# Token blocks of 2, 2, 4, 4, 4 tiles in place of 2, 2, 3, 3, 3, 3, with four down accumulators and a ring of three PSUM banks

## The chip, the cores and the metric

The kernel runs on one core of a Trainium2 chip. The metric is the device time of one execution in microseconds. Before the change the runs took 521.86 us in the median of three (521.49 to 524.5). All compute engines of the core work side by side, each with its own in-order queue: TensorE (PE in the profile, with its weight loads as PEld), VectorE (DVE), ScalarE (ACT), GpSimd (POOL) and SyncE (SP), which issues the DMAs.

## What is computed

Two branches, each added to a residual stream x of 2048 tokens by 448 channels, with layer norms whose shift, scale and gate come from a condition c. The first branch is a long convolution of the tokens with a kernel K, the second a SwiGLU feed-forward network (FFN) of hidden width 1792:

```python
h = layernorm(x) * (1 + ca) + sa
x = x + ga * (conv(h, K) + h * Dskip)
h = layernorm(x) * (1 + cb) + sb
x = x + gb * ((silu(h @ w_gate) * (h @ w_up)) @ w_down)
```

For the inputs at hand the exponents in K are so small that K[l] = m0 + l m1, and the convolution becomes prefix sums over the tokens: a triangular matrix `tri` is multiplied with two products of h, and one row `run` carries what the earlier tokens leave to a tile.

## The kernel before

**Tiles and blocks.** The tokens lie in 16 tiles of 128 (on the partitions). The tiles are grouped in blocks (`BLOCKS`, line 23): 2, 2, 3, 3, 3 and 3 tiles. The FFN is worked block by block (`ffn`, from line 649, called at line 774). The hidden width is cut in 14 pieces f of 128. For each piece, `gate_up` (from line 664) multiplies the 448 channels of the block's tokens with the gate and up weights into two PSUM banks: 22 matmuls (line 678), each with as many columns as the block has tokens, 256 or 384. There are 22 because tokens and weights are kept as two float32r parts, `hhi`/`hlo` and the parts in `gu`. ACT then takes the silu of the gate bank (L684), DVE multiplies it with the up bank (L689, reads PSUM), ACT casts the product to `phi` (L692), and DVE keeps the rest in `plo` (L693). The down weights are split in `wdh` (ACT, L659) and `wdl` (POOL, L660) for each block and piece again. `down` (L704) multiplies them, 3 matmuls of 448 columns for each tile, into one accumulator bank for each tile: `dn0`, `dn1`, `dn2`.

**Order on PE.** PE runs gate_up(f), then down(f - 1), then gate_up(f + 1) and so on (loop at line 706). So the chain silu, product, cast, rest of piece f is meant to run beside PE's next work.

**The next block beside it.** While a block's FFN runs, the tiles of the next block are brought up to it. This work is in stages s0 to s5 for each tile (from line 780): s0 the first norm (DVE, L178 and L180); s1 the products v0 and v1 (POOL, L791 and L792); s2 adds the row `run` to both (DVE L797, POOL L798), casts `vh` (ACT, L801) and keeps the rest `vl` (DVE, L802); s3 the skip term (POOL, L807); s4 the three `tri` matmuls (PE, L813 to L815) into the bank `cv` and a bank `s` of the ring, and an addition (DVE, L816); s5 reads `o` and `s` (ACT L823, DVE L824, L826, L827) and passes `run` on through a small DMA (L825), which the next tile's s2 waits for. Then follow the second norm's statistics (L119, L120), its root for the block's tiles together (a guess on DVE, L125 to L128, Newton's steps on POOL, L134 to L137), the scaled tokens `xn` (DVE, L189), and, behind the last gate_up of the block, the transposes (PE, L196). These put each of the four channel groups k in a bank of the ring, from where ACT and DVE read `hhi` (L198), `fl` (L202 on DVE for k = 0 and 2, L200 on ACT for 1 and 3) and `hlo` (L203).

**What sets the order.** It is written by hand. `TIMES` (line 28) says in which half piece h each stage is emitted: h // 2 is the piece f; an even h stands between gate_up(f) and down(f - 1), an odd one behind down(f - 1). Its first row is for the work beside block 0, the second for that beside block 1, the third for all later blocks. In each row come the root of the first norm, then s0 to s5 for each tile, the root of the second norm, and `xn`. Every engine takes its instructions in this order.

**PSUM.** There are eight banks: four in a ring (`psg`, line 51, handed out in turn by `bank()`), three accumulators, and `cv`; `dn2` also serves the beginning.

**The beginning.** Until about 45 us the kernel's coefficients and the first two tiles are worked out. Block 0 runs while the FFN's weights come in and are split.

Of the kernel before, what the change touches and what calls it, by code (L numbers as in the profile page):

```python
# [17 lines left out]
NT = L // 128          # token tiles  # L18
P = 112                # partitions that the channels are spread over, four on each
NF = F // 128          # tiles of the hidden width  # L20
NP0 = 3                # pieces of the FFN's weights loaded before the branch
NS = 3                 # pieces on their way at a time
BLOCKS = [2, 2, 3, 3, 3, 3]
TILES = [list(range(sum(BLOCKS[:b]), sum(BLOCKS[:b + 1]))) for b in range(len(BLOCKS))]
MB = max(BLOCKS)
# when the root of the next block's first norm, the stages of its tiles, and the root and the shift
# of its second norm run, in half pieces of the hidden width: for the first block, the second, and those that follow
TIMES = (
# [3 lines left out]
)  # L32
EPS = 1e-5
# with exponents per step below this (here: the root of the sum of their squares), exp(l dt A) is
# 1 + l dt A to float32's accuracy for every l < L
# [8 lines left out]
def tile_kernel(ctx, tc, x, a_re, a_im, b_re, b_im, c_re, c_im, log_dt, dskip,  # L44
                wg, wu, wd, c, w_mod, dft, idft, out):
    nc = tc.nc
# [4 lines left out]
    psg = ctx.enter_context(tc.tile_pool(name="psg", bufs=4, space=PS))  # L51
# [16 lines left out]
    # ---- weights of the FFN, one tile of the hidden width at a time: gate and up are kept as  # L68
    # two float32r parts each (for the last 64 channels on top of each other), down whole ----
# [29 lines left out]
    tok = const.tile([128, 1], F32)     # a token's place in its tile  # L99
    run = const.tile([128, 2, D], F32)  # row 0: what the tokens so far leave to a tile, see s1  # L100
# [4 lines left out]
    gm1 = g0                        # the general path works the gates out again  # L105
# [16 lines left out]
    def guess(v, n, tag):  # L122
        """the beginning of 1 / sqrt(v + eps): a first guess from the bits, for Newton's steps"""
        a, w, y, t = (small.tile([128, n], F32, name=q + tag) for q in "awyt")
        ve.tensor_scalar(a, v, EPS, None, op0=OP.add)  # L125
        ve.tensor_scalar(w, v, EPS, -0.5, op0=OP.add, op1=OP.mult)
        ve.tensor_scalar(y.bitcast(I32), a.bitcast(I32), 1, None, op0=OP.logical_shift_right)
        ve.tensor_scalar(y.bitcast(I32), y.bitcast(I32), -1, 0x5F3759DF, op0=OP.mult, op1=OP.add)  # L128
        return w, y, t
# [15 lines left out]
    class Norm:  # L145
        """mean and 1 / deviation of the tokens of a block's tiles"""
# [69 lines left out]
    # the sum over the four channels of a partition  # L216
# [11 lines left out]
    def end_gate():  # L228
        """the sum over the partitions, on every partition"""
        ps = psd.tile([128, 512], F32, name="dn2")[:, 0:D]  # L230
        pe.matmul(ps, ones[0:P, :].to_broadcast([P, 128]), gb[0:P], start=True, stop=True)
        sc.copy(gb, ps)

    def mod_col(col, row, bias):
        """sums over a row's partitions as columns, the last 64 channels twice"""
        pc = bank()
        for q, o in ((0, 0), (1, 0), (2, 0), (3, 0), (3, 64)):
            n = 128 if q < 3 else 64
            pe.matmul(pc[o:o + n, q:q + 1], row[:, q * 128:q * 128 + n], ones[0:row.shape[0], :], start=True, stop=True)
        sc.activation(col, pc[:, 0:4], AF.Identity, bias=bias)  # L240

    def row_of(m):
        """a row of the kernel on every partition"""
        ps = bank()
        for k in range(4):
            pe.matmul(ps[:, k * P:(k + 1) * P], m[:, k:k + 1].to_broadcast([P, 128]), ident[0:P, 0:P],
                      start=True, stop=True)
        return ps[:, 0:D].rearrange("q (k p) -> q p k", k=4)
# [5 lines left out]
    def warm(n):  # L254
        """keeps the tensor engine's clock up while it waits"""
        ps = bank()
        for _ in range(n):
            pe.matmul(ps.rearrange("p (a b) -> p a b", a=4), tri, tri[:, None, :].to_broadcast([128, 4, 128]),
                      start=True, stop=True)
# [4 lines left out]
    with tc.tile_pool(name="pre", bufs=1) as pre, tc.tile_pool(name="wm", bufs=6) as wm:  # L264
# [52 lines left out]
        # all ones, and the steps from a token of the first tile to one of the second  # L317
# [4 lines left out]
        # what the parts of both tiles leave to the third: column 0 at its first token, column 32 for  # L322
        # each step
# [24 lines left out]
        # K[d, l] for small exponents: m0 + l m1, with m0 = sum C dt B and m1 = sum C dt B dt A  # L348
# [37 lines left out]
        # the exponents of one step  # L386
# [10 lines left out]
        # the branch of the first tiles  # L397
# [52 lines left out]
        # v0 of the tiles to come has their own places taken off  # L450
# [6 lines left out]
    def general_conv():  # L457
        hd = dram.tile([L, D], F32, name="hd")
        kd = dram.tile([L, D], F32, name="kd")          # columns in the order (k p)
# [19 lines left out]
        with tc.tile_pool(name="kg", bufs=1) as kg:  # L479
            tr = {n: kg.tile([128, 2, D], F32, name="tr" + n) for n in ("rho", "th", "tc", "wr", "wi", "wn")}  # L480
            with tc.tile_pool(name="ka", bufs=1) as ka:
# [25 lines left out]
                # angles in turns; whole turns of a step (and of LF steps) drop out exactly  # L507
# [12 lines left out]
            with tc.tile_pool(name="ke", bufs=2) as ke, tc.tile_pool(name="kt", bufs=2) as kt:  # L520
# [9 lines left out]
                def powers(n, cnt, hf, d0, re, im):  # L530
                    """exp(l dt A) for the steps l of iot[n]: re and im are [128, DC, cnt]"""
                    sh = [128, DC, cnt]
                    io = iot[n][:, None, :].to_broadcast(sh)
                    th = tr["th" if n == "f" else "tc"][:, hf, d0:d0 + DC][:, :, None].to_broadcast(sh)
                    rh = tr["rho"][:, hf, d0:d0 + DC][:, :, None].to_broadcast(sh)
                    a = kt.tile(sh, F32, name="a" + n)
                    m = kt.tile(sh, F32, name="m" + n)
                    po.tensor_tensor(m, rh, io, op=OP.mult)
                    if n == "c":
                        sc.activation(m, m, AF.Exp, scale=float(LF))  # L540
                    else:
                        sc.activation(m, m, AF.Exp)
                    ve.tensor_tensor(a, th, io, op=OP.mult)
                    frac(a, re)
                    sc.activation(im, a, AF.Sin, scale=TURN)
                    ve.scalar_tensor_tensor(a, a, -1.0, a, op0=OP.mult, op1=OP.max)
                    sc.activation(re, a, AF.Sin, scale=-TURN, bias=half_pi)
                    po.tensor_tensor(im, im, m, op=OP.mult)
                    ve.tensor_tensor(re, re, m, op=OP.mult)

                for d0 in range(0, D, DC):
                    e2 = ke.tile([128, 2, 2, DC, LF], F32, name="e2")
                    e1 = ke.tile([128, 2, 2, DC, LC], F32, name="e1")
                    for hf in range(2):
# [7 lines left out]
                        # re(W e1) and -im(W e1)  # L562
# [15 lines left out]
        # blocks of 512 steps, transformed at the roots of z^512 = i: the real part of a  # L578
        # product's inverse is its low half, the imaginary part its high half
# [64 lines left out]
    def run_blocks(pools, st, first=None):  # L644
# [3 lines left out]
        def ffn(ts, fresh, last, todo):  # L648
# [5 lines left out]
            def split_d(j):  # L654
                if last:            # the gates of the end go into the weights
                    po.tensor_tensor(wdn[j], wdn[j], gb, op=OP.mult)
                hi = hid.tile([128, D], F32R, name="wdh")
                lo = hid.tile([128, D], F32R, name="wdl")
                sc.copy(hi, wdn[j])  # L659
                po.tensor_tensor(lo, wdn[j], f32(hi), op=OP.subtract)  # L660
                wp[j] = hi, lo

            def gate_up(f, nw):
                head = fresh and f == 0     # the tokens come in while it runs
# [8 lines left out]
                def mm(s, lo):  # L673
                    # the parts of the weights that meet each part of the tokens
# [42 lines left out]
            if last:                # one tile after the other  # L717
# [26 lines left out]
        for b, ts in enumerate(TILES):  # L744
            todo = {}
            if b + 1 < len(TILES):
# [18 lines left out]
                for n, (h, *hs) in ((n1, root1), (n2, root2)):  # L765
                    go(h, n.guess, nx)
                    for h in hs:        # on Pool if a step at a time
                        go(h, n.newton, nx, len(hs) > 1, 3 // len(hs))
# [7 lines left out]
    def small_path(pools):  # L776
# [8 lines left out]
        # K * h up to a token at place t of a tile: v0 and v1 are the parts of h at t = 0 and for  # L785
        # each step, so it is sum v0 + t sum v1. Row 0 brings in the tokens before the tile.
# [125 lines left out]
```

## Time and profile before

| what | value |
|---|---|
| median of the runs | 521.86 us (521.49 to 524.5) |
| span of the profiled execution, first to last instruction | 522.0 us |
| mean granted TensorE clock | 0.980 |
| PE busy | 489.4 us (94%) |
| DVE / ACT / POOL busy | 315.5 / 189.0 / 242.4 us |
| block 0, from 45 us to the first gate matmul of block 1 | until 122.7 us |
| block 1 | 122.7 to 188.0 us |
| blocks 2, 3, 4, 5 | begin at 188.0, 271.0, 354.0 and 436.9 us |

A row of the timeline gives start in us, duration in us, engine, line of the kernel, operation, out<-in, shape and count, and in brackets how long the engine had been idle and what released it. A row of the chain of waits gives start, duration, and the engine and line that held the end up. A row of the windows gives, for each engine, the busy time in a stretch, then the granted clock of TensorE and the DMA share. Matmuls overlap one another, so their pace is read from their starts and not from their durations.

### The profile page before, as it was taken

Reading aid. Unit: us, or ns where it says so; the run is one execution under the profiler, and the core shown is the slowest. Engines: PE = TensorE matmul, PEld = TensorE weight load, DVE = VectorE, ACT = ScalarE, POOL = GpSimd, SP = SyncE. Lnnn points to the kernel's source line nnn. Section 1 sums busy time; section 2 is a strip of 40 time slices with the busy share of each in tenths; the row PEclk is TensorE's granted clock in tenths of the full one; section 3 lists DMA queues with packets and bytes.
Section 4 is the critical chain, followed back from the end, with each engine's and each line's share of the span. In section 5 each row is a group of like instructions: output and inputs, shape, how many; then the busy total and the mean of one; then the engine's idle time right before and its main releaser. Section 6 shows DMA issues by size and latency. Waiting matters only on the chain.

```text
span 522.0 us, 7464 instructions
## 1 busy us (share of the span) xinstructions
PE 489.4 (94%) x2747; PEld 454.8 (87%) x2747; DVE 315.5 (60%) x598; ACT 189.0 (36%) x388; POOL 242.4 (46%) x293
## 2 busy tenths in 40 slices
PE   7768988789989899999999999999999999999995
PEld 4345877679979899999999999999999999999995
DVE  3889889986877764577285466557367538221122
ACT  4346743534333342333243233333233324232221
POOL 1676494552566513565312566311548433434430
PEclk9879999998998989999999999999999999999999
DMA  7995554402000020000003000003000001000001
GB/s 209 277 217 158 157 168 140 122 22 89 0 2 1 2 89 0 1 1 3 1 5 101 0 2 0 2 0 107 1 0 2 0 1 54 1 1 0 2 0 60
DMA packets 25862, 26.08 MB, mean 50 GB/s; under 512 B 2232, under 2 KB 25144, under 8 KB 25816
## 3 DMA queue, kind: packets, MB, share of 16 engines
q1 hardware_dynamic: 25816, 25.52, 17.2%
q8 instruction: 23, 0.38, 0.3%
q14 instruction: 23, 0.19, 0.1%
HBM read 21.80 MB, written 3.67 MB: 49 GB/s over the span
## 4 chain that ended last, share of the span: by engine, by line
PE 73%; DVE 15%; issue 4%; ACT 2%; POOL 2%; DMA 2%; SPq 1%; DVEq 0%; ACTq 0%; POOLq 0%
PE bank L678 46%; PE dn L704 23%; DMA bi<-in_A_B_im_dram 2%; DVE plo L693 2%; DVE gu L95 1%; PE bank L196 1%; DVE xn L189 1%; DVE scr L359 1%; PE dn L415 1%; DVE stb L119 1%; DVE v L797 1%; DVE gu L93 1%; DVE x L816 1%; DVE x L827 1%; DVE wr L368 1%
## 5 line engine op out<-in xcount | busy, mean ns | idle before, releaser
L678 PE MATMUL bank<-hhi,gu 128*128 128x384 f32 (+1 forms) x1169 | 212.6, 321 | 0.5 <-DVE gu L95 0.4
L678 PEld LDWEIGHTS bank<-hhi,gu 128*128 128x128 f32 x1169 | 191.9, 189 | 4.4 <-DVE gu L95 0.6
L660 POOL TENSOR_TENSOR wdl<-wd,wdh 128x448 fp32r<-128x448 f32 x84 | 104.0, 1241 | 191.8 <-ACT wdh L659 183.2
L678 PE MATMUL bank<-hlo,gu 128*128 128x384 f32 (+1 forms) x668 | 131.9, 319 | 0.0
L689 DVE TENSOR_TENSOR p<-p,bank 128x384 f32<-128x384 f32 (+1 forms) x84 | 42.6, 507 | 126.9 <-PE bank L678 122.5
L678 PEld LDWEIGHTS bank<-hlo,gu 128*128 128x128 f32 x668 | 110.1, 189 | 0.0
L692 ACT CAST phi<-p 128x384 fp32r<-128x384 f32 (+1 forms) x84 | 40.1, 477 | 160.2 <-DVE p L689 160.1
L693 DVE TENSOR_TENSOR plo<-p,phi 128x384 fp32r<-128x384 f32 (+1 forms) x84 | 54.5, 649 | 40.5 <-ACT phi L692 40.5
L704 PE MATMUL dn<-wdh,phi 128*128 128x448 f32 x224 | 61.8, 376 | 3.5 <-ACT phi L692 3.4
L684 ACT ACTIVATE p<-bank 128x384 f32<-128x384 f32 (+1 forms) x83 | 37.8, 455 | 71.3 <-PE bank L678 71.2
L704 PE MATMUL dn<-wdh,plo 128*128 128x448 f32 x224 | 60.9, 372 | 2.7 <-DVE plo L693 2.7
L704 PE MATMUL dn<-wdl,phi 128*128 128x448 f32 x224 | 61.0, 373 | 1.5 <-POOL wdl L660 1.5
L659 ACT CAST wdh<-wd 128x448 fp32r<-128x448 f32 x84 | 47.6, 566 | 31.3 <-PE dn L704 28.3
L704 PEld LDWEIGHTS dn<-wdh,plo 128*128 128x128 f32 x224 | 42.5, 191 | 7.8 <-DVE plo L693 4.2
L704 PEld LDWEIGHTS dn<-wdl,phi 128*128 128x128 f32 x224 | 42.9, 192 | 6.1 <-POOL wdl L660 2.3
L704 PEld LDWEIGHTS dn<-wdh,phi 128*128 128x128 f32 x224 | 40.4, 192 | 5.9 <-ACT phi L692 4.5
L791 POOL TENSOR_TENSOR v<-h,gm 128x448 f32<-128x448 f32 x14 | 16.4, 1169 | 12.7 <-DVE h L180 12.7
L801 ACT CAST vh<-v 128x448 fp32r<-128x448 f32 x14 | 7.9, 567 | 33.3 <-DVE v L797 33.3
L798 POOL TENSOR_TENSOR v<-v,run 1x448 fp32r<-1x448 f32 x14 | 17.4, 1240 | 2.3 <-DMA run<-run 1.3
L792 POOL TENSOR_TENSOR v<-h,g 128x448 fp32r<-128x448 f32 x14 | 18.2, 1297 | 0.0
L807 POOL TENSOR_TENSOR h<-h,gd 128x448 f32<-128x448 f32 x14 | 17.6, 1260 | 0.0
L189 DVE TENSOR_SCALAR xn<-x,mvb,yb 128x448 f32<-128x448 f32 (+1 forms) x28 | 16.1, 643 | 2.2 <-POOL yb L137 2.2
(182 smaller groups left out, 462.3 us busy)
## 6 DMA issues: line engine op xcount, KB each, us to landing
wmt<-in_w_mod_dram SPq DMA_DIRECT2D x6, 784.0 KB
x<-in_A_u_dram SPq DMA_DIRECT2D x16, 224.0 KB
out_dram<-x SPq DMA_DIRECT2D x16, 224.0 KB
wd<-in_B_w_down_dram SPq DMA_DIRECT2D x14, 224.0 KB
raw<-in_B_w_gate_dram SPq DMA_DIRECT2D x14, 192.0 KB
raw<-in_B_w_up_dram SPq DMA_DIRECT2D x14, 192.0 KB
raw<-in_B_w_gate_dram SPq DMA_DIRECT2D x14, 64.0 KB
raw<-in_B_w_up_dram SPq DMA_DIRECT2D x14, 64.0 KB
```

Of the source, the lines that this page charges most:

```text
L189: ve.tensor_scalar(xn[i][:, o:o + n], src[:, a:a + n], *n2.of[i], op0=OP.subtract, op1=OP.mult)
L659: sc.copy(hi, wdn[j])
L660: po.tensor_tensor(lo, wdn[j], f32(hi), op=OP.subtract)
L678: pe.matmul(ps[s][:, 0:n], w[:, s, a], (hlo if lo else hhi)[:, k, 0:n], start=not lo and a == 0, stop=lo and k == 3)
L684: sc.activation(p[:, 0:n], ps[0][:, 0:n], AF.Silu)
L689: ve.tensor_tensor(p[:, 0:n], p[:, 0:n], ps[1][:, 0:n], op=OP.mult)
L692: sc.copy(hi[:, 0:n], p[:, 0:n])
L693: ve.tensor_tensor(lo[:, 0:n], p[:, 0:n], f32(hi[:, 0:n]), op=OP.subtract)
L704: pe.matmul(dn[q][:, 0:D], u[:, cs], v, start=f == 0 and z == 0, stop=f == NF - 1 and z == 2)
L792: po.tensor_tensor(v1, h, gm1, op=OP.mult)
L798: po.tensor_tensor(v1[0:1], f32(v1[0:1]), run[0:1, 1, :], op=OP.add)
L807: po.tensor_tensor(h, h, gd, op=OP.mult)
```

## The change

The last twelve tiles are grouped by four, in three blocks in place of four. `MB` becomes 4, so that the tiles `hhi`, `hlo`, `p`, `phi`, `plo` grow from 384 to 512 columns, there are 8 buffers for x in place of 6 and 4 for `xn` in place of 3. A fourth accumulator `dn3` needs a bank, and the ring is cut to three. `TIMES` has four tiles in its second and third row, at a regular distance of four half pieces. A last line makes room on chip by a smaller scratch for DMAs that GpSimd would issue; the kernel has none. Comments are left out of the new file, which shifts its line numbers by two.

```diff
-BLOCKS = [2, 2, 3, 3, 3, 3]
+BLOCKS = [2, 2, 4, 4, 4]
...
 TIMES = (
     ((3, 3, 4, 4), (6, 8, 8, 9, 11, 11), (12, 14, 15, 17, 20, 20), (21, 22, 23, 23), (24, 25)),
-    ((3, 4), (6, 8, 9, 10, 10, 11), (10, 10, 13, 13, 15, 16), (15, 16, 18, 18, 21, 21), (21, 22, 22, 23), (24, 24, 24)),
-    ((3, 3, 3, 3), (7, 8, 8, 10, 10, 10), (10, 13, 13, 14, 14, 15), (14, 17, 17, 18, 18, 19), (19, 20, 21, 22), (24, 24, 24)),
+    ((3, 4), (5, 6, 6, 7, 8, 8), (8, 9, 10, 11, 12, 12), (12, 13, 14, 15, 16, 16), (16, 17, 18, 19, 20, 20),
+     (21, 22, 22, 23), (24, 24, 24, 24)),
+    ((3, 3, 3, 3), (5, 6, 6, 7, 8, 8), (8, 9, 10, 11, 12, 12), (12, 13, 14, 15, 16, 16), (16, 17, 18, 19, 20, 20),
+     (20, 21, 22, 23), (24, 24, 24, 24)),
 )
...
-    psg = ctx.enter_context(tc.tile_pool(name="psg", bufs=4, space=PS))
+    psg = ctx.enter_context(tc.tile_pool(name="psg", bufs=3, space=PS))
...
-    nc = bacc.Bacc("TRN2", target_bir_lowering=False, num_devices=1)
+    nc = bacc.Bacc("TRN2", target_bir_lowering=False, num_devices=1, dynamic_dma_scratch_size=1024)
```

## The prediction

> **What bounds the kernel now.** I read the page first, then the windows cut at the first gate matmul of each block, then the chain of waits, and at last the timeline of the places where the chain leaves PE.
>
> ```profile
> span 522.0 us, 7464 instructions
> PE 489.4 (94%) x2747; PEld 454.8 (87%) x2747; DVE 315.5 (60%) x598; ACT 189.0 (36%) x388; POOL 242.4 (46%) x293
> ```
>
> ```profile
> 122.70:188.00 65.30, 61.93 (x415) 57.54 (x414) 50.45 (x107) 24.31 (x54) 33.98 (x39) 0.95 0.06 19
> 188.00:271.00 83.00, 83.00 (x457) 80.97 (x456) 46.05 (x88) 27.64 (x54) 36.71 (x50) 1.00 0.05 15
> ...
> 354.00:436.90 82.90, 82.90 (x457) 80.74 (x456) 48.15 (x90) 27.37 (x54) 37.69 (x51) 1.00 0.05 18
> 436.90:522.00 85.10, 79.70 (x435) 77.27 (x433) 21.76 (x38) 21.35 (x42) 31.08 (x27) 1.00 0.05 18
> ```
>
> Blocks 2 to 4 have PE busy without a gap at clock 1.00, DVE a little over half of the time. There PE's pace is the time. Block 1 is different: 65.30 us, PE not always busy, clock 0.95, DVE 50.45 of 65.30. The profiled span (522.0) and the median (521.86) agree, so I add to 522.0.
>
> PE's pace comes from the chain of waits (a piece with 256 tokens, one with 384):
>
> ```profile
> 129.24 2.57 PE bank L678 x22
> 131.81 1.23 PE dn L704 x6
> ...
> 201.64 1.82 PE dn L704 x9
> 203.46 3.89 PE bank L678 x22
> ...
> 209.17 3.89 PE bank L678 x22
> 266.20 1.31 PE bank L196 x12
> ```
>
> A 384-token piece takes 209.17 - 203.46 = 5.71 us: 22 gate/up matmuls in 3.89 (176.8 ns each) and 9 down matmuls in 1.82 (202 ns each). With 256 tokens it is 2.57 (116.8 ns each) and 1.23, so 3.80 a piece. Fourteen pieces of 5.71, nine `tri` matmuls of about 0.2 and 1.31 of transposes make 83.1, the window's 83.0: a block's edge costs nothing beside its work.
>
> **The change part by part.**
>
> *Wider gate and up matmuls.* Gate/up matmuls in the last twelve tiles go from 4 x 14 x 22 = 1232 of 384 columns to 3 x 14 x 22 = 924 of 512. The work of 448 columns (down, transposes, `tri`) is per tile and stays. The timeline shows one run of 512-column matmuls on the same type, the warming ones, at clock 1.00; each row begins with the start of another of them:
>
> ```profile
> 13.63 0.85 PE L258 MATMUL bank<-tri 128*128 128x512 f32 x3
> 13.86 0.85 PE L258 MATMUL bank<-tri 128*128 128x512 f32 x3
> 14.09 0.84 PE L258 MATMUL bank<-tri 128*128 128x512 f32 x3
> 14.32 1.07 PE L258 MATMUL bank<-tri 128*128 128x512 f32 x4
> ```
>
> ```profile
> 13.50:14.00 0.50, 0.50 (x4) 0.41 (x3) 0.50 (x2) 0.00 (x0) 0.00 (x0) 1.00 0.99 287
> ```
>
> (14.32 - 13.63) / 3 = 230 ns; I take 229, since 448 columns at 202 and the step from 384 to 448 (25 ns for 64) lead there too. A third more columns than 384 would be 236 at proportional pace. So 22 x 0.229 = 5.04 where pro rata it is 3.89 x 4/3 = 5.19: 0.148 a piece, times 42 pieces: **-6.2 us**. Ends: 0 (236 ns) and, from 512 columns at the slope 448 to 384 without any fixed part (about 0.4 ns a column, some 213 ns), -20.
>
> *One tile more is prepared in block 1.* Blocks 2 and 3 prepare 8 tiles where blocks 2 to 4 prepared 9; its 0.6 of `tri` and 0.44 of transposes leave them: **-1.0 us**.
>
> *Block 1 with four tiles.* This is the term that decides. Block 1 still has 256 tokens and 14 pieces of 3.80, but must bring up four tiles. The marks are the starts of the subtraction `vl`, once for each tile:
>
> ```profile
> 143.40 0.87 DVE L802 TENSOR_TENSOR vl<-v,vh 128x448 fp32r<-128x448 f32 x1 [0.63 <-ACT vh L801]
> 155.74 0.63 DVE L802 TENSOR_TENSOR vl<-v,vh 128x448 fp32r<-128x448 f32 x1 [0.69 <-ACT vh L801]
> 155.75 0.47 PE L813 MATMUL cv<-vh,tri 128*128 128x448 f32 x1 [1.44 <-ACT vh L801]
> 169.39 0.63 DVE L802 TENSOR_TENSOR vl<-v,vh 128x448 fp32r<-128x448 f32 x1 [0.63 <-ACT vh L801]
> ```
>
> 12.34 and 13.65 us lie between them, though by `TIMES` (half pieces 9, 13, 18) only 2 and 2.5 pieces do, 7.6 and 9.5 us of PE. PE waits for the stages (row at 155.75). What fills the distance is DVE's queue, one after the other: product, cast wait, rest of two pieces, L816, L824, L826, L827, statistics, next tile's L178 and L180, L797, wait for `vh`, `vl`. Beside POOL some of these are stretched:
>
> ```profile
> 146.61 0.63 DVE L816 TENSOR_TENSOR x<-h,x 128x448 f32<-128x448 f32 x1 [1.05 <-POOL h L807]
> 152.09 1.13 POOL L798 TENSOR_TENSOR v<-v,run 1x448 fp32r<-1x448 f32 x1
> 152.37 1.21 DVE L693 TENSOR_TENSOR plo<-p,phi 128x256 fp32r<-128x256 f32 x1 [0.47 <-ACT phi L692]
> 153.50 1.55 DVE L797 TENSOR_TENSOR v<-v,run 1x448 f32<-1x448 f32 x1
> 157.38 0.43 DVE L693 TENSOR_TENSOR plo<-p,phi 128x256 fp32r<-128x256 f32 x1 [0.47 <-ACT phi L692]
> 168.15 0.61 DVE L797 TENSOR_TENSOR v<-v,run 1x448 f32<-1x448 f32 x1
> ```
>
> The same L693 takes 0.43 alone and 1.21 while POOL's L798 runs, L797 0.61 and 1.55. In the new `TIMES` the marks stand at half pieces 6, 10, 14 and 18: three distances of exactly 2 pieces, with the same DVE work as in the 12.34. Bounds for one: 12.34 less 0.78, 0.94 and the 1.05 wait is 9.6; above 13.65. I take 12.0, near the first distance, which has the same content; a little is taken off because s3 now stands ahead of POOL's next L660. PE offers 2 x 3.80 + 0.6 = 8.2 for it, so DVE stays behind and PE waits in each.
>
> Before the first mark lies the same time as before (143.40 - 122.7 = 20.7): a fourth column in the first norm's statistics and root, but one piece less. The last mark has its old place (18), and behind it come the same four pieces: 188.0 - 169.39 = 18.6, plus the fourth tile's `xn`:
>
> ```profile
> 179.34 3.66 DVE L189 TENSOR_SCALAR xn<-x,mvb,yb 128x448 f32<-128x448 f32 x6 [0.95 <-POOL yb L137]
> ```
>
> (3.66 / 3 = 1.2), and 1.5 for the shorter ring (product, cast, rest and `fl` follow `xn`, and the last transposes wait for them, next part): 21.3. So block 1 is 20.7 + 3 x 12.0 + 21.3 = 78.0, against 65.3: **+12.7 us** (5.5 to 17.7 by the bounds). Queued behind DVE are L689 and L693 of each piece, and PE's next down and gate matmuls wait for those.
>
> *Three banks.* The order of the changed program shows the ring: gate, up, then the four transposes take banks 0, 1, 2, 0, 1, 2. The third group waits for L689 on the up bank, the fourth for L198 and L202 to empty the first group's bank. Before, it had a bank of its own.
>
> ```profile
> 266.04 1.47 PE L196 MATMUL bank<-ident,xn 128*128 128x128 f32 x12
> 266.30 0.55 DVE L689 TENSOR_TENSOR p<-p,bank 128x384 f32<-128x384 f32 x1 [1.23 <-PE bank L196]
> 266.89 0.51 ACT L692 CAST phi<-p 128x384 fp32r<-128x384 f32 x1 [2.05 <-DVE p L689]
> 267.44 0.56 DVE L693 TENSOR_TENSOR plo<-p,phi 128x384 fp32r<-128x384 f32 x1 [0.58 <-ACT phi L692]
> 268.01 0.68 DVE L202 TENSOR_SCALAR p<-bank,cb1c,sbc 128x384 f32<-128x384 f32 x1
> ```
>
> L202 ends 2.65 us after the transposes' start. For 512 columns the four steps grow by about 0.5 (their growth from 256 to 384 columns, 0.13, 0.10, 0.14, 0.14): 3.15. Twelve transposes take 1.31, so PE stands 1.8 at the edges 2 to 3 and 3 to 4, and behind the transposes in its queue the last two down groups and the next block's gate matmuls. A stall of this size can cost clock behind it:
>
> ```profile
> 180.00:184.00 4.00, 2.50 (x20) 1.95 (x18) 3.53 (x8) 0.64 (x2) 1.66 (x2) 0.98 0.00 0
> 184.00:188.00 4.00, 4.00 (x15) 3.59 (x13) 3.60 (x8) 3.61 (x7) 0.31 (x1) 0.59 0.00 0
> 184.31 3.85 PE dn L704 x12
> ```
>
> After 1.5 us of idleness the clock was 0.59 and twelve down matmuls took 3.85 instead of 12 x 0.202 = 2.43, 1.4 lost. I charge it at one of the two edges: 2 x 1.8 + 1.4 = **+5.0 us** (0 to 6.4). At the edge of block 0:
>
> ```profile
> 117.91 0.99 PE L196 MATMUL bank<-ident,xn 128*128 128x128 f32 x7 [1.07 <-DVE xn L189]
> 118.66 0.82 PE L704 MATMUL dn<-wdh,phi 128*128 128x448 f32 x2
> 119.35 0.54 DVE L202 TENSOR_SCALAR p<-bank,cb1c,sbc 128x256 f32<-128x256 f32 x1
> ```
>
> the fourth group waits until 119.89 and the down matmuls begin 0.2 later, at 120.1 in place of 118.66: **+1.4 us** (0 to 1.4). Inside the pieces the ring makes gate(f + 2) wait for L827 where an s4 stands in piece f: in blocks 0 and 1 that falls inside waits already charged, in the wide blocks L827 has two pieces (15 us) for it.
>
> *At nothing.* Splits of down weights fall from 84 to 70 on ACT and POOL, off the path. SP issues 4 loads of x at a time; for blocks 3 and 4 they queue behind the stores of the same buffers, and are needed one piece (7.5 us) later. If that cover went, DVE would stand in L119 and L689 behind it. In the beginning the fourth transposes wait too; the cover is DVE's splitting of weights, and without it some 0.4 us. The end has one tile more to add, each beside the next tile's down matmuls.
>
> **Sum.** 522.0 - 6.2 - 1.0 + 12.7 + 5.0 + 1.4 = **533.9 us**.
>
> **The rivals.**
>
> *Not slower: the fourth tile fits in block 1.* DVE is idle for 65.3 - 50.45 = 14.9 us there, more than the 12.0 charged for a whole tile. Then block 1 grows by PE's own 1.0 alone, and the sum is 522.0 - 7.2 + 1.0 + 6.4 = 522.2. Against it: idle time between dependent steps was there before too, and the distance was still 12.3. It decides at 9.8 us a tile: below it the total stays within 1%.
>
> *512 columns run without the fixed part.* If a gate/up matmul took 216 ns in place of 229, it would be 924 x 13 = 12 us less: 521.9. For it: the slope from 384 to 448 columns; against it: the four rows above. The Trainium skill, "TensorE: Matmul & The Clock Gate", section "Wait — 56ns, not 53.3ns?", gives 2.5 ns beside the columns at 2.4 GHz, 215.7 ns for 512 columns; its estimate for 384 is 162.5, where this trace has 176.8, so it does not hold here.
>
> *Wider is only proportional* (236 ns): the -6.2 is gone, 540.1.
>
> *DVE and the clock are worse:* three distances of 13.65 (+5.0) and the clock lost at both edges (+1.4): 540.3. The Trainium skill, same page, section "A second HAM failure mode: psum-queue depth-cycling", speaks for it: waits for PSUM banks can make the clock swing. Blocks 2 to 4 at 1.00 show no such swing with four banks.
>
> **How the numbers follow.** Forecast 0.52; only proportional 0.10; worse 0.13; fourth tile fits 0.11; no fixed part 0.06; both of these last (about 510) 0.08. One per cent (516.8 to 527.2) is about what a measurement tells from no change. Faster is the last case, 0.08; within it are the two single ones, 0.17; slower the rest, 0.75. The range 521 to 543 leaves out the case at 510 and the two bad cases together (546.5); the forecast's own range is 527 to 541.
>
> **What would show it.** Block 1's window near 78 us, with `vl` starts some 12 us apart and PE's L813 waiting for `vh` at each of four tiles. Gate/up pieces of 512 tokens near 5.04 us. At the edges of the wide blocks 12 transposes, a gap of about 1.8 us ended by DVE L202, then 4 more. It is wrong if block 1 stays below 72 us, or if the wide pieces take 4.75 or 5.19.

## The result, and the profile after

The changed kernel takes 543.36 us in the median of four runs (542.84 to 547.14), the kernel before, on the same chip, 522.93 (521.49 to 524.5). The ratio is 1.0396, with a 95% interval of 1.0354 to 1.0437: the change makes the kernel 4% slower. The forecast was 533.9, and its range ended at 543. Line numbers of the changed kernel are those of the kernel before plus two (L693 is now L695).

The head of the page of the changed kernel, and its windows, cut again at the first gate matmul of each block (duration, then busy time of PE, PEld, DVE, ACT and POOL, then TensorE's granted clock):

```profile
span 541.3 us, 6691 instructions
...
PE 494.4 (91%) x2439; PEld 415.2 (77%) x2439; DVE 318.7 (59%) x561; ACT 175.7 (32%) x340; POOL 222.2 (41%) x255
```

```profile
124.92:204.78 79.86, 65.07 (x422) 60.45 (x421) 60.59 (x126) 26.12 (x56) 40.38 (x43) 0.91 0.06 18
204.78:316.85 112.07, 110.55 (x505) 93.23 (x505) 64.39 (x104) 32.60 (x56) 44.22 (x55) 1.00 0.04 13
316.85:428.92 112.07, 110.55 (x506) 93.21 (x505) 65.99 (x106) 32.07 (x55) 44.65 (x56) 1.00 0.05 17
428.92:541.30 112.38, 105.94 (x477) 88.96 (x475) 26.25 (x40) 24.31 (x41) 28.96 (x26) 0.99 0.05 18
```

Set beside the windows of the kernel before, this gives the whole difference of the spans, 541.3 - 522.0 = 19.3:

| stretch | before | after | difference | forecast |
|---|---|---|---|---|
| start to block 1 | 122.7 | 124.9 | +2.2 | +1.4 |
| block 1 | 65.3 | 79.9 | +14.6 | +12.7 |
| the last twelve tiles | 334.0 | 336.5 | +2.5 | -2.2 |
| sum | 522.0 | 541.3 | +19.3 | +11.9 |

So the loss sits in block 1, as forecast, and the wide blocks, which were to give something back, give nothing. The time of this profiled execution is 543.13, which is 1.8 above its span; the forecast added to a span of 522.0 as if it were a time. Of the distance from 533.9 to 543.1, 7.4 us are terms of the sum and 1.8 this base.

**The wide blocks.** The chain of waits of the changed kernel shows their pieces, and the edge between blocks 2 and 3 (start, duration, what held the end up):

```profile
217.49 5.13 PE bank L680 x22
222.63 2.43 PE dn L706 x12
225.06 5.13 PE bank L680 x22
...
308.43 0.68 DVE p L691
309.13 0.63 ACT phi L694
309.79 0.69 DVE plo L695
310.48 0.81 DVE p L204
311.33 0.66 PE bank L198 x4
311.99 4.86 PE dn L706 x24
```

A 512-column matmul steps by 5.13 / 22 = 233.2 ns, not 229; four thirds of the old 176.8 would be 235.7. The gain is 924 x 2.5 ns = 2.3 us, not 6.2. At the edge PE leaves the chain for DVE and ACT, exactly in the order that the forecast gave: product, cast, rest, then `fl` (L204), and only then the last four transposes. The window of 112.07 less 14 pieces of 7.565, 12 `tri` matmuls (2.4) and 16 transposes (1.75) leaves 2.0 us of standstill at such an edge. The 24 down matmuls behind it run at 202.5 ns: no clock is lost.

**Block 1.** The marks `vl`, and the PE, POOL and DVE rows around the second of them, in the timeline of the changed kernel:

```profile
146.20 0.85 DVE L804 TENSOR_TENSOR vl<-v,vh 128x448 fp32r<-128x448 f32 x1 [0.63 <-ACT vh L803]
157.70 0.79 DVE L804 TENSOR_TENSOR vl<-v,vh 128x448 fp32r<-128x448 f32 x1 [0.69 <-ACT vh L803]
170.22 0.79 DVE L804 TENSOR_TENSOR vl<-v,vh 128x448 fp32r<-128x448 f32 x1 [0.69 <-ACT vh L803]
182.75 0.79 DVE L804 TENSOR_TENSOR vl<-v,vh 128x448 fp32r<-128x448 f32 x1 [0.69 <-ACT vh L803]
```

```profile
157.72 0.47 PE L815 MATMUL cv<-vh,tri 128*128 128x448 f32 x1 [0.80 <-ACT vh L803]
159.53 0.47 PE L816 MATMUL bank<-v,tri 128*128 128x448 f32 x1 [1.34 <-POOL v L800]
```

```profile
154.09 1.16 POOL L793 TENSOR_TENSOR v<-h,gm 128x448 f32<-128x448 f32 x1 [4.76 <-DVE h L182]
155.21 1.33 POOL L794 TENSOR_TENSOR v<-h,g 128x448 fp32r<-128x448 f32 x1
156.50 1.51 POOL L662 TENSOR_TENSOR wdl<-wd,wdh 128x448 fp32r<-128x448 f32 x1
157.97 1.50 POOL L800 TENSOR_TENSOR v<-v,run 1x448 fp32r<-1x448 f32 x1
159.44 1.32 POOL L809 TENSOR_TENSOR h<-h,gd 128x448 f32<-128x448 f32 x1
```

```profile
160.80 1.56 DVE L818 TENSOR_TENSOR x<-h,x 128x448 f32<-128x448 f32 x1 [1.04 <-POOL h L809]
```

The distances are 11.50, 12.52 and 12.53. In the last two, the split of a down weight (POOL, L662) stands in POOL's queue between v1 and its row (L800). So L800 ends 1.5 us later, PE waits 1.34 in L816 behind a wait for `vh`, and DVE waits 1.04 in L818 for the skip term. The forecast had POOL's next split behind s3, and did not count the one ahead of L800. It also put the whole distance down to DVE's queue. In these two distances the chain goes over to POOL and back: L793 starts when DVE's `h` is done (L182), POOL works v0, v1, the split, v1's row and the skip term one after the other (154.09 to 160.76), and DVE's L818 waits for the last of them. Before the first mark lie 21.3 us, between the marks 36.6, behind the last 22.0: 79.9. TensorE's granted clock is 0.91 over the block, where it was 0.95 before.

**The end.** Behind the end of PE's last matmul the changed kernel's span lasts 6.5 us more, that of the kernel before 5.4: +1.1. There is one store more in the last block (four in place of three), but the run *What the 512 columns read* below has four as well, and lasts 5.4 us there. So the number of stores is not shown to be the reason; over the profiles of the changed tiling this stretch varies from 5.4 to 6.5.

### The profile page after: what moved, and what is told of

It is laid out like the page before. It is cut to its first block, busy times and chain, and to the rows that moved or that the text cites. A ratio compares the mean times of both kernels' runs of the same rounds, so it can differ in the third digit from the quotient of the medians.

```text
span 541.3 us, 6691 instructions
## 1 busy us (share of the span) xinstructions
PE 494.4 (91%) x2439; PEld 415.2 (77%) x2439; DVE 318.7 (59%) x561; ACT 175.7 (32%) x340; POOL 222.2 (41%) x255
## 4 chain that ended last, share of the span: by engine, by line
PE 69%; DVE 12%; POOL 7%; issue 5%; DMA 3%; ACT 2%; SPq 1%; POOLq 0%; ACTq 0%; DVEq 0%
PE bank L680 43%; PE dn L706 21%; POOL wdl L662 2%; DVE plo L695 2%; DVE xn L191 1%; DVE scr L361 1%; POOL v L800 1%; DMA x<-in_A_u_dram 1%; DMA dsk<-in_A_Dskip_dram 1%; PE bank L215 1%; DMA wd<-in_B_w_down_dram 1%; POOL v L794 1%; POOL v L793 1%; PE dn L417 1%; DVE gu L97 1%
## 5 line engine op out<-in xcount | busy, mean ns | idle before, releaser
L680 PE MATMUL bank<-hhi,gu 128*128 128x512 f32 (+1 forms) x973 | 206.9, 352 | 2.3 <-DVE x L829 1.2
L680 PEld LDWEIGHTS bank<-hhi,gu 128*128 128x128 f32 x973 | 162.6, 190 | 28.9 <-DVE x L829 1.4
L662 POOL TENSOR_TENSOR wdl<-wd,wdh 128x448 fp32r<-128x448 f32 x70 | 87.2, 1249 | 164.6 <-ACT wdh L661 160.9
L680 PE MATMUL bank<-hlo,gu 128*128 128x512 f32 (+1 forms) x556 | 126.5, 349 | 0.0
L691 DVE TENSOR_TENSOR p<-p,bank 128x512 f32<-128x512 f32 (+1 forms) x70 | 40.5, 579 | 138.9 <-PE bank L680 134.3
L680 PEld LDWEIGHTS bank<-hlo,gu 128*128 128x128 f32 x556 | 92.6, 188 | 15.4
L694 ACT CAST phi<-p 128x512 fp32r<-128x512 f32 (+1 forms) x70 | 37.4, 535 | 160.5 <-DVE p L691 160.5
L695 DVE TENSOR_TENSOR plo<-p,phi 128x512 fp32r<-128x512 f32 (+1 forms) x70 | 52.3, 748 | 36.9 <-ACT phi L694 36.9
L686 ACT ACTIVATE p<-bank 128x512 f32<-128x512 f32 (+1 forms) x69 | 35.4, 512 | 80.4 <-PE bank L680 80.4
L793 POOL TENSOR_TENSOR v<-h,gm 128x448 f32<-128x448 f32 x14 | 16.3, 1166 | 69.7 <-DVE h L182 69.7
L800 POOL TENSOR_TENSOR v<-v,run 1x448 fp32r<-1x448 f32 x14 | 20.3, 1453 | 0.4
L809 POOL TENSOR_TENSOR h<-h,gd 128x448 f32<-128x448 f32 x14 | 20.3, 1453 | 0.0
L215 PE MATMUL bank<-wmt,cs 112*128 112x448 f32 (+1 forms) x32 | 16.8, 683 | 2.9 <-DMA wmt<-in_w_mod_dram 2.9
```

What stands on the lines that cost most here:

```text
L215: pe.matmul(ps[0:rows, 0:D], cs[:, k:k + 1].to_broadcast([P, rows]), w[k], start=k == 0, stop=k == 3)
L680: pe.matmul(ps[s][:, 0:n], w[:, s, a], (hlo if lo else hhi)[:, k, 0:n], start=not lo and a == 0, stop=lo and k == 3)
L686: sc.activation(p[:, 0:n], ps[0][:, 0:n], AF.Silu)
L691: ve.tensor_tensor(p[:, 0:n], p[:, 0:n], ps[1][:, 0:n], op=OP.mult)
L694: sc.copy(hi[:, 0:n], p[:, 0:n])
L695: ve.tensor_tensor(lo[:, 0:n], p[:, 0:n], f32(hi[:, 0:n]), op=OP.subtract)
```

## The experiments

**The ring alone.** The kernel before, with three banks in the ring and nothing else changed:

```diff
-    psg = ctx.enter_context(tc.tile_pool(name="psg", bufs=4, space=PS))
+    psg = ctx.enter_context(tc.tile_pool(name="psg", bufs=3, space=PS))
```

> The kernel before (blocks 2, 2, 3, 3, 3, 3) with the ring cut to three banks and nothing else. If the ring costs what the prediction says, the fourth group of transposes waits for L202 at each of the five edges: about 1.3 us at the first two and, with 384 columns (L202 ends 2.65 us after the transposes begin, nine of them take 1.0), about 1.65 at the other three, together 7.6 us: near 530.5 against 522.9. Rival: these waits are hidden by what stands behind them and the ring costs nothing, 523; then all of the loss in the changed kernel is block 1.

Measured: 535.48 us against 523.42, ratio 1.0228 (1.0184 to 1.0272). The windows of its blocks 1 to 3, and a row of its timeline from the beginning:

```profile
126.72:194.33 67.61, 63.27 (x415) 58.41 (x414) 50.63 (x107) 24.63 (x54) 34.19 (x38) 0.93 0.05 18
194.33:279.48 85.15, 83.81 (x457) 81.24 (x456) 46.50 (x89) 28.00 (x54) 36.92 (x50) 1.00 0.05 15
279.48:364.26 84.78, 83.44 (x456) 80.93 (x456) 47.62 (x91) 27.97 (x54) 36.94 (x51) 1.00 0.05 17
```

```profile
49.18 0.69 PE L196 MATMUL bank<-ident,xn 128*128 128x128 f32 x2 [1.62 <-DVE fl L202]
```

Each edge of a block costs about 2 us (85.15 and 84.78 against 83.0, block 1 67.6 against 65.3), close to the 1.8 of the forecast. The rest, 4.0 us, lies before block 1, where the same wait stands twice: at the edge of block 0, and in the beginning, where the fourth transposes wait for `fl`; 0.8 of it is there before the first transpose (45.33 in place of 44.49), so ahead of any such wait. In all the ring costs 12 us here with five edges, against the 7.6 expected, which had left out the beginning. The changed kernel has four edges; what they cost there is the next run.

**The tiling without the edges' wait.** The changed kernel, with the fourth transposes of each edge in the bank of `cv`:

```diff
...
-            ps = bank()
+            ps = psd.tile([128, 512], F32, name="cv") if spare and k == 3 else bank()
...
-                at(NF - 1, 0, transposes, nx, new_fl)
+                at(NF - 1, 0, transposes, nx, new_fl, True)
```

> The changed kernel with the last of the four transposed groups of a block's edge put into the bank cv, which is idle there, so that the ring of three acts as four at the edges. If the ring is the cause, the 2.0 us at each of the two wide edges, about 1.3 at the edge of block 1 and 1.0 at that of block 0 go: 6.3 us less, about 537 against 543.4. Rival: the wait goes over to the next bank (the gate bank of the next block) or to the down matmuls, 543.

Measured: 536.63 against 523.42, ratio 1.027 (1.0225 to 1.0315). The windows of block 1 and the first wide block:

```profile
122.77:201.06 78.29, 65.02 (x422) 60.64 (x421) 60.27 (x126) 25.38 (x56) 40.60 (x42) 0.91 0.06 19
201.06:311.40 110.34, 110.34 (x506) 93.23 (x505) 65.81 (x106) 33.81 (x59) 43.99 (x55) 1.00 0.04 13
```

PE now has no gap in a wide block, and that saves 1.7 us an edge. At its own pace twelve tiles in such blocks are hardly quicker than in blocks of three, and block 1 is still 13 us longer than before. So the ring's waits at the edges are worth about 7 of the 20 us, and 13 stay with these waits gone: they are block 1's.

**Three tiles in block 1.** The changed kernel without the stages s0 to s5 of tile 7, the last of the four:

```diff
                     for h, g in zip(hs, st):
-                        go(h, g, i)
+                        if (b, q) != (1, 3):
+                            go(h, g, i)
```

> The changed kernel without the stages s0 to s5 for the last tile that block 1 prepares (tile 7: its first branch is left out of the result, and its carry). If a tile costs one distance of the chain of DVE and POOL, block 1 shrinks by 12.5 us to about 67, total near 531. Rival: the fourth tile fits beside the others and costs PE's 0.6 alone, and what makes block 1 long is its edge and the late loads of x: 543.

Measured in a single run: 535.13. Its block 1 and its first and last mark:

```profile
125.98:197.75 71.77, 62.18 (x419) 58.15 (x418) 53.92 (x118) 25.24 (x54) 34.35 (x39) 0.95 0.06 20
```

```profile
145.70 0.85 DVE L805 TENSOR_TENSOR vl<-v,vh 128x448 fp32r<-128x448 f32 x1 [0.63 <-ACT vh L804]
...
169.74 0.80 DVE L805 TENSOR_TENSOR vl<-v,vh 128x448 fp32r<-128x448 f32 x1 [0.69 <-ACT vh L804]
```

Taking away the fourth tile takes 8.1 us off the block, between the two expectations. The distance of 12.5 is gone, but the two pieces that stood in it remain: behind the last mark the block now needs 28.0 us in place of 22.0. Two pieces are 7.6; about 1.5 of them comes back through the clock, which was 1.00 there in place of 0.92. A further 1.6 lies before the first mark (19.7 in place of 21.3), and this one profile does not say why. So a tile more costs its distance less the PE work that fits into it.

**No split of the down weights in block 1.** The changed kernel without POOL's subtractions in block 1; the down matmuls there take the high part in place of the low one, as many as before:

```diff
...
-                po.tensor_tensor(lo, wdn[j], f32(hi), op=OP.subtract)
-                wp[j] = hi, lo
+                if ts is not TILES[1]:
+                    po.tensor_tensor(lo, wdn[j], f32(hi), op=OP.subtract)
+                wp[j] = hi, hi if ts is TILES[1] else lo
```

> The changed kernel with POOL's split of the down weights left out in block 1 alone (the cast part stands in for the rest, so the result is not exact). If the exclusive use of a port by DVE and POOL sets the distance of 12.5 us between tiles, it falls to about 10.3 (L818 0.62 in place of 1.56, no wait for L800 and L809), block 1 to about 73, total 536. Rival: DVE's own queue alone sets it, the distance stays at 12 to 12.5 and the time at 542 to 543.

Measured in a single run: 532.22, beyond what either theory gave it. Its block 1 and its marks:

```profile
125.30:194.63 69.33, 61.99 (x422) 57.34 (x421) 55.20 (x126) 26.04 (x56) 24.00 (x29) 0.98 0.07 21
```

```profile
144.53 0.85 DVE L805 TENSOR_TENSOR vl<-v,vh 128x448 fp32r<-128x448 f32 x1 [0.63 <-ACT vh L804]
155.09 0.86 DVE L805 TENSOR_TENSOR vl<-v,vh 128x448 fp32r<-128x448 f32 x1 [0.63 <-ACT vh L804]
...
176.23 0.85 DVE L805 TENSOR_TENSOR vl<-v,vh 128x448 fp32r<-128x448 f32 x1 [0.63 <-ACT vh L804]
```

Groups of DVE's instructions between 125 and 180 us (busy time, mean ns of one, idle time before), of the changed kernel and then of this run:

```profile
L818 DVE TENSOR_TENSOR x<-h,x 128x448 f32<-128x448 f32 x3 | 4.7, 1557 | 2.1 <-POOL h L809 2.1
```

```profile
L819 DVE TENSOR_TENSOR x<-h,x 128x448 f32<-128x448 f32 x4 | 2.5, 614 | 0.0
```

Block 1 falls by 10.5 us to 69.3, with four tiles. All distances are 10.56, and between the marks DVE's queue alone is now the chain. That is 4.9 us less between the marks; 2.0 fall away before the first and 3.6 behind the last, where PE no longer waits for v1's row and the clock holds (0.98 over the block in place of 0.91). The same addition takes 614 ns where POOL is not working beside it and 1557 where it is, and DVE no longer waits for POOL in front of it. The Trainium skill, "SBUF — State Buffer", section "Who interferes with whom", says that a DVE instruction with two inputs in SBUF and a GpSimd instruction that reads SBUF lock each other out, while one with a single SBUF input runs beside it. The rows agree: L818 has two SBUF inputs, and L691, which reads `p` and a PSUM bank, is not stretched anywhere: all 14 of block 1 in the changed kernel take 405 to 422 ns, beside POOL or not. How much of the gain is the split's place in POOL's queue and how much the lock, no run separates.

**What the 512 columns read.**

```diff
...
+                            if n == 512:
+                                o = o.rearrange("p (a b) -> p a b", a=4)
+                                m = (hlo if lo else hhi)[:, k, 0:128][:, None, :].to_broadcast([128, 4, 128])
...
```

> The changed kernel, with one edit: the moving operand of each 512-column gate and up matmul is the first tile's 128 columns of the tokens, read four times over, so each still writes 512 columns of its bank but the values of the other three tiles are wrong; in time nothing else moves. The theory (a fixed part is spread over more columns, 229 ns a step, and something in the way 512 columns are read adds the 4 ns that the profile shows): the 22 matmuls of a wide piece take 5.04 us in place of 5.13, a block 110.8 in place of 112.1, the run 543.4 - 3 x 1.3 = 539.5. The rival (the step grows with the columns and there is no fixed part to spread): 5.13 us, 112.1 a block and 543.4, as before the edit.

Measured in a single run: 542.37. Its first wide block:

```profile
204.99:317.05 112.06, 110.54 (x505) 93.20 (x505) 64.44 (x104) 32.57 (x56) 44.20 (x55) 1.00 0.04 13
```

No more than a hundredth of a microsecond a block is won (112.06 against 112.07). The pace doesn't depend on which columns are read, so that does not explain the 4 ns. That there is next to no fixed part is read from the steps at three widths, further below.

**Both repairs of the changed kernel.** The split of the run below on DVE in block 1, beside the transposes in `cv`. The line edited for the beginning belongs to a path that these inputs don't take, so the beginning is unchanged, and its part of the expectation isn't tested here.

```diff
...
-                po.tensor_tensor(lo, wdn[j], f32(hi), op=OP.subtract)
+                (ve if ts is TILES[1] else po).tensor_tensor(lo, wdn[j], f32(hi), op=OP.subtract)
```

> The changed kernel, with its two costs repaired as far as a few lines do it: the fourth channel group's transposes use the bank of the convolution (that of cv), at the block edges and in the beginning, so that nobody waits there for the third bank back; and in block 1 alone the low part of the down weights is subtracted on DVE in place of POOL. The theory (in block 1 a POOL subtraction of 1.5 us holds DVE as well, so 0.45 to 0.65 us on DVE itself is cheaper): block 1 from 79.9 to about 75 us, the marks of vl some 11.5 apart in place of 12.5; the edges 1.7 shorter each as in the run with that edit alone; the beginning 1 to 2 shorter; in all 543.4 - 4.8 - 2 x 1.7 - 1.5 - 0.5 = 533, that is still 10 slower than the kernel before, since the fourth tile in block 1 is not paid back. The rival (DVE is the bound of block 1 whoever holds it, and 14 more operations of 0.9 us make up for what POOL no longer does): block 1 stays at 80, and the run is 537 or 538.

Measured: 535.5 against 523.65, ratio 1.0218 (1.0148 to 1.0289). Block 1, and two of the moved subtractions, the first beside POOL's skip term (L809):

```profile
124.48:200.97 76.49, 65.40 (x422) 60.08 (x421) 64.17 (x140) 25.08 (x56) 25.57 (x28) 0.93 0.06 19
```

```profile
158.24 1.56 DVE L662 TENSOR_TENSOR wdl<-wd,wdh 128x448 fp32r<-128x448 f32 x1
...
165.68 0.62 DVE L662 TENSOR_TENSOR wdl<-wd,wdh 128x448 fp32r<-128x448 f32 x1
```

Block 1 is 1.8 us shorter than with POOL's splits (78.29), and the marks lie 12.2 apart, between the 11.5 of the theory and the 12.5 of before. The run too lies between the two: 535.5, where the theory without its beginning gives some 534.5 and the rival 537. Between the marks DVE no longer waits for POOL and its own queue is the chain, but it has 14 operations more, and four of them take 1.56 us beside POOL's other work.

**The same split on DVE in the kernel before**, with the diff just shown:

> The kernel before, with one edit: in block 1 alone the low part of the down weights is subtracted on DVE in place of POOL. If POOL's subtractions hold DVE there, block 1 (65.3 us, of which PE was busy in 61.9) gets 2 us shorter, and the run is 521.4 against 523.4. The rival: with three tiles to prepare block 1 isn't bound by DVE, so nothing is won, or DVE's 14 added operations cost up to 3 us: 523.4 to 526.

Measured: 520.69 (10 runs) against 523.65, ratio 0.9946 (0.9917 to 0.9975). Block 1:

```profile
122.60:184.80 62.20, 59.51 (x415) 54.79 (x414) 51.08 (x118) 22.93 (x52) 19.32 (x24) 1.00 0.06 20
```

Block 1 is 3 us shorter than 65.3, though DVE has 14 operations more. The marks are 12.2 and 12.9 us apart in place of 12.3 and 13.7, which is 0.9; about 1.5 is the clock at the block's edge, where twelve down matmuls take 2.5 us in place of 4.0 (clock 1.00 over the block in place of 0.95). This version is faster than both kernels.

**An earlier chain in block 1 of the kernel before**, with the split on DVE:

```diff
...
-    ((3, 4), (6, 8, 9, 10, 10, 11), (10, 10, 13, 13, 15, 16), (15, 16, 18, 18, 21, 21), (21, 22, 22, 23), (24, 24, 24)),
+    ((3, 4), (5, 6, 6, 6, 8, 8), (9, 10, 10, 10, 12, 12), (13, 14, 14, 14, 17, 17), (18, 19, 20, 21), (24, 24, 24)),
```

> The kernel before, with the edit of the run beside it (block 1's low part of the down weights on DVE) and another list of half pieces for block 1: each tile's stages s1 to s4 come two to four half pieces sooner and the next tile's stage closer behind, s3 together with s2. It looks for a kernel that beats both. The theory (in block 1 the chain of three tiles ends at the same time as PE, so an earlier chain lets PE run at its own pace): block 1 at 61 to 62 us in place of 65.3, the run at 519.5 to 520.5. The rival (PE gets in front of work that isn't ready, and waits inside its queue for vh): 523 to 526.

Measured: 525.17 against 523.65, ratio 1.0031 (1.0004 to 1.0059): the gain of the split is lost again. Block 1 lasts from 121.87 to 188.63, 66.8 us. Here too the marks lie 12.2 apart, and PE waits 1.89, 1.88 and 0.52 us for `vh` in front of the three tiles' `tri` matmuls. A place in the list is not a time: with the chain at its own pace, an earlier place only makes PE wait in front of it.

**The beginning.** The run with the edges' transposes in `cv`, and the fourth transposes of the beginning in the bank of the fourth accumulator:

```diff
...
-        transposes(TILES[0], lambda: pre.tile([128, MB * 128], F32, name="fl", bufs=2))
+        transposes(TILES[0], lambda: pre.tile([128, MB * 128], F32, name="fl", bufs=2), "dn3")
```

> The changed kernel with the fourth channel group's transposes in a bank of their own at the block edges (as in the run with that edit alone, 536.6) and now in the beginning too, where the call that this input runs puts them in the bank of the fourth down accumulator, which is free until block 2. What is left of the change is then its tiling alone, without the third bank's waits. The theory (the first gate matmul starts at 51 to 52 us in place of 47 to 49 because the fourth transposes wait for fl, and the clock is lower behind it): the first gate matmul at 47.5 to 49.3, block 1 starts 1 to 2 us sooner than 122.8, the run at 535. The rival (block 0 waits for its weights and for DVE either way, so the beginning's wait is hidden, and what differs between profiles is the chance of the loads): block 1 at 122.8, the run at 536.6.

Measured: 534.05 against 523.9, ratio 1.0187 (1.0151 to 1.0222). In its profile the wait is gone, and from the first transpose to the first gate matmul it takes 4.2 us (45.58 to 49.81) in place of 6.5 in the changed kernel (45.22 to 51.71). But block 1 begins at 124.50, 78.9 after the first transpose, where the run without this edit had 78.1 and the kernel before 78.2. What hides the gain is the clock at the edge of block 0: the twelve down matmuls there take 4.1 us at a granted clock of 0.58 (120.42 to 124.50), and 2.5 at 1.00 in the run without the edit (120.26 to 122.77). Up to that edge, from the first transpose of the beginning to the first one of the edge, this run takes 72.4 us. The kernel before, and its two runs above with the split on DVE in block 1, take 71.8 to 72.2, the seven profiles with three banks in the beginning 72.3 to 74.3, in the mean 73.5. So the wait is not wholly hidden behind block 0: it costs about 1.4 us, as the theory has it. The median is 2.6 lower than without the edit, but that is a comparison across chips.

**The split on DVE in blocks 0 and 1 of the kernel before** (`ts in TILES[0:2]` in the diff above):

> The kernel before with the low part of the down weights on DVE in blocks 0 and 1, where the run with block 1 alone gave 520.7. The theory (POOL's subtraction holds DVE in block 0 as it does in block 1, and DVE was busy in 44.8 of the 50 us of block 0's middle): block 0 up to 2 us shorter, 519. The rival (in block 0 DVE splits the gate and up weights as well and is the bound itself, and 14 operations of 0.6 us are added to it while POOL holds it less often): block 0 up to 4 us longer, 521 to 525.

Measured: 518.27 (516.03 to 518.7) against 523.9, ratio 0.9877 (0.9837 to 0.9917). Groups of DVE's instructions between 66 and 116 us, of the kernel before and then of this run:

```profile
L693 DVE TENSOR_TENSOR plo<-p,phi 128x256 fp32r<-128x256 f32 x10 | 9.1, 908 | 0.5 <-ACT phi L692 0.5
L95 DVE TENSOR_TENSOR gu<-raw,gu 64x256 fp32r<-64x256 f32 x9 | 8.0, 890 | 0.3
```

```profile
L660 DVE TENSOR_TENSOR wdl<-wd,wdh 128x448 fp32r<-128x448 f32 x11 | 6.8, 621 | 0.1
L693 DVE TENSOR_TENSOR plo<-p,phi 128x256 fp32r<-128x256 f32 x10 | 6.1, 608 | 0.5 <-ACT phi L692 0.5
L95 DVE TENSOR_TENSOR gu<-raw,gu 64x256 fp32r<-64x256 f32 x9 | 5.5, 607 | 0.3
```

In this stretch DVE takes on 6.8 us of subtractions and gets back some 300 ns, in the mean, on each L693 and L95, 5.5 in all; block 1 begins at 119.46 in place of 122.73. This is the fastest kernel of the study.

**The changed tiling with every repair**: the last two edits, made in the changed kernel together with the transposes in `cv`.

> The changed tiling with every repair that the runs so far found: the fourth transposes in banks of their own at the edges and in the beginning (534.05 with these alone), and the low part of the down weights on DVE in blocks 0 and 1, which took the kernel before from 523.9 to 518.3. What is then left of its distance to the kernel before with that same edit is the price of the tiling by itself. The theory (block 0 gains 3 as it did in the kernel before; in block 1, where DVE is the bound, only 1.8 as in the run with both repairs of the changed kernel): 529, so 11 slower than the kernel before with that edit. The rival (the two tilings gain the same, 5.6): 528.4 or less, and if block 1 came down to the pace of the run without any subtraction there (69 us) about 522.

Measured: 530.33 against 524.06, ratio 1.0149 (1.0093 to 1.0204). Block 1:

```profile
118.91:194.92 76.01, 65.06 (x422) 60.07 (x421) 64.24 (x140) 25.20 (x56) 25.54 (x28) 0.93 0.06 19
```

On equal terms the tiling is 12 us slower than 2, 2, 3, 3, 3, 3 (530.33 and 518.27, from two chips whose runs of the kernel before agree within 0.2). Block 1 lasts 76.0 us against 63.3, and the twelve tiles behind it 332.5 against 333.9. What four tiles to a block cost in block 1 is nine times what they save afterwards.

## Why the prediction was wrong, point by point

The direction and the place were right, the size was not. The step that failed is *Wider gate and up matmuls*: its 229 ns gave -6.2, and the matmuls step by 233.2, so -2.3. Its evidence was three steps of the warming matmuls, read from starts rounded to 0.01 us, so 230 with an error of some 3 ns. The next three steps of the same run (14.32 to 15.00 us) come to 227, so a 512-column matmul of another kind, at the same clock of 1.00, is no measure for gate and up; why it is quicker, no run shows. From there I went to 229, led by the small step from 384 to 448 columns. That one is a comparison of two different matmuls: gate and up on one side, down on the other. From 256 columns over 384 to 512, the steps of the gate matmuls are 116.8, 176.8 and 233.2: 60.0 and 56.4 for 128 columns, so there is next to no fixed part to spread. The first of these differences stood in the prediction's own rows, and leads to 236.8. With *Wider is only proportional* (0.10) I had the case, but at too low a chance. That is 3.9 of the 7.4 us.

*Block 1*: PE waited for `vh` at each of the four tiles, and 12.0 for a distance was near (11.5, 12.5, 12.5); the block came out at 79.9 in place of 78.0, with 0.6 more before the first mark, 0.6 between the marks and 0.7 behind the last. The account of the distance was right in half. DVE's queue alone sets the first one; in the other two half of the chain is POOL's queue, with a split of the down weights between v1 and its row. That 12.0 came so near has a reason that the prediction does not give: the 12.34 that it started from already held a split and the skip term on POOL (L816 waits 1.05 for L807). I had seen POOL stretch L693 and L797, and used that only for a lower bound. Without the splits the distance is 10.56, and the block 10.5 us shorter.

*Three banks*: the mechanism was right, with 2.0 at each wide edge in place of 1.8; the lost clock that I charged at one of them did not come. 4.0 in place of 5.0. *At nothing*: the end cost 1.1 more in this profile, not shown to be a cost of the change. The wait in the beginning costs some 1.4 by the run that takes it away, though hardly in this profile (72.3 us up to the edge of block 0, 72.1 before). The start to block 1 cost 2.2 in place of 1.4, of which the first transpose alone, at 45.22 in place of 44.49, is 0.7; over the runs it varies from 43.8 to 46.1. The *1.0* for one tile less in blocks 2 and 3 was not measured by itself; with it, the terms of the last twelve tiles add up to -2.3 - 1.0 + 4.0 + 1.1 = +1.8, against +2.5.

*The rivals.* *The fourth tile fits* was wrong: its point was 9.8 us a tile, and a tile took 11.5 to 12.5, and 10.56 even without the splits. Its argument, DVE's idle 14.9 us, counted idle time that stands between dependent steps. *No fixed part* was wrong by the 233.2. *Worse* was wrong: the distances, 12.2 in the mean, lie nearer to 12.0 than to its 13.65, and the clock held at the wide edges; clock was lost in block 1 instead (0.91 in place of 0.95). The Trainium skill, "TensorE: Matmul & The Clock Gate", section "A second HAM failure mode: psum-queue depth-cycling", speaks of a clock that swings where PE waits for banks; with three banks these blocks still had 0.99 to 1.00, so a wait of 2 us in 112 shows no such swing here.

## What to carry to other kernels

Regrouping work by larger blocks moves the preparation of the first large block into a smaller one before it: cost that block by the chain of the engines that prepare (here DVE's queue and POOL's), not by the engine that bounds the rest. A third more columns for the same weights is worth something only if the trace shows a fixed part in the same instruction at two sizes; measure that before counting on it. And where DVE and POOL work beside one another on operations with two SBUF inputs, compare POOL's price with what it takes from DVE: moving 28 subtractions of 1.1 to 1.9 us from POOL to DVE, which was the busier engine, made the kernel before 1.2% faster.

## What the runs showed of the hardware that was not expected

- A 512-column float32r matmul with its own weight load steps by 233.2 ns at granted clock 1.00, whether its moving operand is 512 columns of SBUF or 128 columns read four times (112.06 and 112.07 us a block).
- One and the same DVE operation takes 614 ns or 1557 beside POOL, while one that reads a PSUM bank and one SBUF tile keeps to 405 to 422. A subtraction of 0.62 us on DVE can replace one of 1.1 to 1.9 on POOL and shorten the block, though DVE is the busier engine: by 3 us in block 1 of the kernel before, by 1.8 with the fourth tile, where DVE's queue is the chain.
- The clock behind stalls of about a microsecond is not the same from profile to profile: the twelve down matmuls at the edge of block 0 took 2.5 us at granted clock 1.00 (120.26 to 122.77) in the changed kernel with the transposes in `cv`, and 4.1 at 0.58 (120.42 to 124.50) in the one that differs from it in the beginning alone, each behind waits of 1.0 and 1.1 us for `xn`. These 1.6 us are as much as the term that was forecast at that place; what decides between the two, no run shows.
